# Attention, soft experts and a gated layer on one core: first loads in longer runs, two weights moved into attention

## The chip, the core and the metric

The kernel runs on one core of a Trainium2 chip. The core has TensorE (PE, matrix products, with its weight loads listed as PEld), VectorE (DVE), ScalarE (ACT), GpSimd (POOL) and SyncE (SP, which here only issues DMAs), an on-chip memory of 128 partitions (SBUF), and accumulators that only PE, DVE and ACT reach (PSUM). The metric is the time of one execution in device microseconds (us). Each engine takes its instructions strictly in the order in which the program lists them; a waiting instruction holds up everything behind it on its engine.

## The reference

Three layers follow each other; the output of one is the input of the next.

```
# attention: 4 batches, 12 heads, 448 tokens, 64 wide
scores = q @ k.T / 8;  masked above the diagonal
attn   = softmax(scores);  x = attn @ v            # -> x: 1792 x 768
# soft experts: 8 experts with 4 slots each, 1024 wide
logits = x @ phi                                   # 1792 x 32
d = softmax(logits over tokens);  slot_in = d.T @ x
slot_out[e] = relu(slot_in[e] @ w1[e]) @ w2[e]
x = softmax(logits over slots) @ slot_out
# gated layer: 1536 wide
out = (sigmoid(x @ w_gate) * (x @ w_val)) @ w_out
```

q, k, v, phi, w1 and w2 are 32-bit floats. The three gated weights come as 64-bit floats; the kernel reads them as 32-bit words and makes 32-bit floats of them on the chip.

## The kernel before

**Attention** works on 24 pairs of heads (six pairs per batch). q, k and v come in 12 groups of four heads, two pairs each. For a pair, PE turns q and k round (tile psT), ACT writes the scaled high half of them in 16 bits and DVE the low half (qT), PE makes the scores (psS), DVE masks them and finds row maxima (nm), ACT takes the exponentials (P), PE turns those round (psP), ACT or DVE copies them to PT, and PE multiplies with v (psV). The scale comes from sums of squares: `first_squares` for group 0, `squares_1` for group 1, both on DVE and ACT; from group 2 on POOL makes them (tiles sq and sqr), and a small product (psq) spreads the result. Group 0's q and k are fetched by `load_first`, one DMA per head, in runs of 256 bytes (a row of 64 floats).

**Experts.** Their weights are 32 tiles of 1.5 MB (two for w1, two for w2 of each expert), read by SP through `load_w` in the order of the list `worder` into a ring of buffers, `ring`: 3 of pool wpC and `NA` of pool wpA, 10 in all, filled during attention. When attention's own memory comes free, five more join the ring. The gated layer is cut into six units of 256 columns; a unit's three weights (o = w_out, v = w_val, g = w_gate) are 1.5 MB each too, and unit 0's three stand in `worder` ahead of expert 6. Right after expert 5, ACT (`a1`, `a2`) and DVE (`d1`, `d2`) make floats of these three tiles, in that order per tile, and the o tile is then split in two 16-bit halves: its largest value (`absw`) goes through a product of ones (`one`, tile amx on PE) and `pow2` (four short DVE instructions that make a power of two and its inverse) before `whi` and `wlo` write the halves.

**Gated layer.** For each unit, `psg` multiplies the experts' result with the g and v weights, `mv` finds the largest values, `one2` spreads them (amx), `pw2` makes powers of two, `gh` and `fld` fold the product, `sth` and `stl` store it in 16 bits (st). Then for each batch `gv` makes gate and value (psg, psv), ACT the sigmoid (sg), DVE the product (hs), ACT and POOL its halves (hhi, hlo), `outp` the products with w_out (pso), and ACT, DVE and POOL add them into oacc. The weights of the next unit are read and converted meanwhile.

**What sets the order.** Attention and the gated layer are each recorded as a list of operations with a cost, dependencies and a due time, and `Plan.play` puts them in order: of the operations that an engine could start within `WAIT` of the earliest, the one due first. The tables `SHIFT` (attention) and `GSHIFT` (gated layer) move due times by kind of operation; `SLACK`, `MARGIN`, `WAIT` and their `A` versions set the rest. The plan only sets an order: on the chip nothing is held until a planned time. The experts between them are ordered by the framework's scheduler. `keep_warm` puts products of ones (psf) that nobody reads where PE would be idle: around the end of attention and at the start of the gated layer.

Of the kernel before, what the change touches and what calls it, by code (L numbers as in the profile page):

```python
# [8 lines left out]
F32 = mybir.dt.float32  # L9
F16 = mybir.dt.float16  # L10
I32 = mybir.dt.int32
# [90 lines left out]
def kernel(  # L102
# [41 lines left out]
    for g, (b, h0, n) in enumerate(GRP):  # L144
        for o in range(0, n, 2):
# [17 lines left out]
    GSHIFT = {('a1', 1): 23.4, ('a1', 2): -6.21, ('a1', 3): 117.66, ('a1', 4): -5.02, ('a1', 5): 53.58, ('a2', 1):  # L163
              20.66, ('a2', 2): 118.34, ('a2', 3): 123.22, ('a2', 4): 79.78, ('a2', 5): 4.11, ('absw',): 36.12,
              ('addp', 1): 9.2, ('addp', 2): -5.3, ('addp', 3): -47.55, ('addp', 4): 58.74, ('am',): 1.36, ('am2',):
              -23.99, ('d1', 1): -180.16, ('d1', 2): 54.75, ('d1', 3): -2.65, ('d1', 4): -1.62, ('d1', 5): 30.01,
              ('d2', 1): 9.59, ('d2', 2): -33.11, ('d2', 3): -32.37, ('d2', 4): 8.67, ('d2', 5): 0.27, ('evict', 0):
              -148.33, ('evict', 1): -68.2, ('evict', 2): -111.03, ('evict', 3): -19.74, ('evict', 4): -31.48,
              ('evict', 5): 19.57, ('fl',): -9.57, ('fld',): 25.66, ('gh',): -29.78, ('gv', 0): -10.56, ('gv', 1):
              -235.77, ('gv', 2): -71.57, ('gv', 3): 21.32, ('gv', 4): 9.31, ('gv', 5): 8.04, ('hhi', 0): -461.87,  # L170
              ('hhi', 1): 83.0, ('hhi', 2): 5.44, ('hhi', 3): 25.33, ('hhi', 4): -7.65, ('hhi', 5): 9.17, ('hlo', 0):
              -0.95, ('hlo', 3): -9.74, ('hlo', 4): 42.9, ('hlo', 5): 20.64, ('hsv', 0): 17.3, ('hsv', 1): -5.98,
              ('hsv', 2): 0.18, ('hsv', 3): -20.78, ('hsv', 4): 18.54, ('hsv', 5): 4.2, ('ld', 1): -6.69, ('ld', 2):
              23.28, ('ld', 3): -32.29, ('ld', 4): -2.0, ('ld', 5): 39.32, ('mv',): -42.04, ('one',): -118.12,
              ('one2',): -17.53, ('outp', 0): 65.58, ('outp', 1): 1.02, ('outp', 10): 136.03, ('outp', 11): -0.62,
              ('outp', 12): -6.35, ('outp', 2): -3.63, ('outp', 3): 123.94, ('outp', 4): -8.45, ('outp', 5): -18.09,
              ('outp', 6): 218.04, ('outp', 7): -1.03, ('outp', 8): 231.97, ('outp', 9): 108.01, ('psg',): -384.17,
              ('pw',): -22.44, ('pw2',): -103.76, ('sig', 0): -240.48, ('sig', 1): -4.63, ('sig', 2): 27.87, ('sig',
              3): -144.49, ('sig', 4): -20.28, ('sig', 5): 17.06, ('sth', 0): -26.98, ('sth', 1): -11.12, ('sth', 2):
              -2.93, ('sth', 3): -40.58, ('sth', 4): -4.7, ('sth', 5): -0.58, ('stl', 0): 3.56, ('stl', 1): -0.2,  # L180
              ('stl', 2): 25.38, ('stl', 3): 8.1, ('stl', 4): -61.65, ('stl', 5): 13.43, ('store', 0): -10.25,
              ('store', 1): 15.69, ('store', 10): 2.55, ('store', 11): 55.39, ('store', 12): 11.05, ('store', 13):
              2.24, ('store', 2): 10.3, ('store', 3): 3.04, ('store', 4): -40.57, ('store', 5): 29.87, ('store', 6):
              7.57, ('store', 7): 43.43, ('store', 8): -4.75, ('store', 9): 49.48, ('whi',): -12.54, ('wlo',): 19.95}
    NFILL = 20
    AE = 9
    SQN = 32
    ASLACK, AMARGIN, AWAIT = 1.317, 1.41, 0.087
    PERIOD = 7.8
# [1114 lines left out]
```

## Time and profile before

| | us |
|---|---|
| three runs: median (lowest to highest) | 519.91 (519.75 to 521.16) |
| the profiled execution | 519.79 |
| its span in the profile | 518.0 |
| PE busy | 470.9 (91%) |
| DVE busy | 378.0 (73%) |
| ACT busy | 341.4 (66%) |
| POOL busy | 277.9 (54%) |

The span has four parts: the start until some 20 us, attention until 207, the experts until 300, the gated layer to the end. Shares of the whole span say little, since each part has another limit. An engine's idle time matters only if the part's limiting engine waits for it.

### The profile page before, as it was taken

What the parts mean: (1) busy time and instruction counts of PE and PEld (TensorE: products, weight loads), DVE (VectorE), ACT (ScalarE), POOL (GpSimd) and SP (SyncE); (2) the same over time, 40 slices, a digit from 0 to 9 for tenths busy, and PEclk for the clock granted to TensorE, in tenths of its full rate; (3) what the DMA queues carried; (4) which work ended last, traced back from release to release, by engine and by line L of the source; (5) the groups of instructions that cost most, each with busy time, mean ns of one, the idle gap of its engine ahead of it and who ended that gap; (6) DMA issues with size and microseconds to landing.
All of it is one profiled execution on the core that took longest, in us unless ns stands there. A gap on an engine that the chain in (4) does not pass through costs nothing.

```text
span 518.0 us, 12116 instructions
## 1 busy us (share of the span) xinstructions
PE 470.9 (91%) x4516; PEld 293.0 (57%) x4516; DVE 378.0 (73%) x920; ACT 341.4 (66%) x759; POOL 277.9 (54%) x371
## 2 busy tenths in 40 slices
PE   3899999999999999999837578999999998999997
PEld 2667767767667776655412234555455554555554
DVE  3889888989988987621055049899798998978564
ACT  3788887989887886111081059999897897686330
POOL 3088777787768812000000007249699997997530
PEclk9999999999999999999985999999999999999999
DMA  6866776762767357899999993360553320300145
GB/s 149 200 167 190 202 218 156 176 186 62 220 154 191 123 154 279 331 416 424 410 409 424 412 395 139 114 253 0 163 204 121 139 106 1 124 0 1 53 178 196
DMA packets 87531, 101.55 MB, mean 196 GB/s; under 512 B 68656, under 2 KB 68912, under 8 KB 85424
## 3 DMA queue, kind: packets, MB, share of 16 engines
q1 hardware_dynamic: 86544, 100.55, 57.4%
q8 instruction: 35, 0.57, 0.5%
q10 hardware_dynamic: 928, 0.23, 0.2%
q14 instruction: 24, 0.20, 0.1%
HBM read 95.26 MB, written 5.51 MB: 195 GB/s over the span
## 4 chain that ended last, share of the span: by engine, by line
PE 54%; POOL 15%; DMA 12%; DVE 6%; ACT 6%; issue 6%; SPq 1%; POOLq 0%; ACTq 0%; DVEq 0%
PE pso L244 11%; PE psP L244 8%; PE psS L244 8%; PE psV L244 7%; DMA w<-in_moe_w_gate_dram 5%; POOL hlo L244 5%; POOL oacc L244 5%; DMA w<-in_moe_w_dram 5%; POOL sq L244 4%; PE so L1069 3%; PE psT L244 3%; PE psh L1056 3%; PE psY L244 2%; PE psX L244 2%; ACT w L244 2%
## 5 line engine op out<-in xcount | busy, mean ns | idle before, releaser
L244 POOL TENSOR_TENSOR hlo<-hs,hhi 128x448 f16<-128x448 f32 x47 | 69.8, 1494 | 124.7 <-ACT hhi L244 124.6
L244 PEld LDWEIGHTS <-hhi 128*128 128x128 f16 x672 | 65.2, 98 | 51.1 <-issue 7.9
L244 ACT ACTIVATE P<-psS,nm 128x384 f32<-128x384 f32 (+3 forms) x168 | 82.1, 505 | 11.4 <-DVE nm L244 8.7
L244 PE MATMUL pso<-wh,hhi 128*128 128x384 f16 x336 | 82.7, 326 | 1.0 <-ACT oacc L244 0.5
L244 POOL TENSOR_TENSOR oacc<-oacc,ev 128x384 f32<-128x384 f32 x56 | 76.4, 1381 | 11.7 <-ACT ev L244 10.3
L244 PE MATMUL pso<-wh,hlo 128*128 128x384 f16 x336 | 81.6, 326 | 0.9 <-POOL hlo L244 0.9
L244 PE MATMUL pso<-wl,hhi 128*128 128x384 f16 x336 | 82.4, 326 | 0.0
L244 DVE CUSTOM_DVE_ANT_0 psS<-psS,cmaskq,sc 128x128 f32<-128x128 f32 (+2 forms) x144 | 62.8, 487 | 3.1 <-PE psS L244 2.4
L244 DVE SCALAR_TENSOR_TENSOR oacc<-pso,osc,oacc 128x384 f32<-128x384 f32 x84 | 50.1, 611 | 18.5 <-PE pso L244 18.2
L244 DVE SCALAR_TENSOR_TENSOR w<-w 128x1536 int32<-128x1536 int32 x30 | 62.0, 2067 | 0.7 <-ACT w L244 0.7
L244 PE MATMUL psP<-ident,P 128*128 128x128 f32 x384 | 59.4, 282 | 1.3 <-ACT P L244 1.3
L244 POOL TENSOR_TENSOR sq<-sq 112x512 bf16<-112x512 bf16 (+1 forms) x80 | 51.1, 639 | 6.0
L244 PEld LDWEIGHTS psP<-ident,P 128*128 128x128 f32 x384 | 42.9, 142 | 15.2 <-issue 8.8
L244 ACT COPY PT<-psP 128x512 f32<-128x512 f32 x83 | 46.7, 587 | 6.3 <-PE psV L244 5.2
L244 PE MATMUL psS<-qT,qT 64*64 64x256 f16 (+3 forms) x1008 | 48.9, 294 | 1.5 <-ACT qT L244 0.7
L244 ACT ACTIVATE w<-w 128x1536 int32<-128x1536 uint16 (+1 forms) x30 | 49.3, 1647 | 1.3 <-DMA w<-in_moe_w_gate_dram 1.3
L244 PE MATMUL psV<-PT,v 128*64 128x448 f32 (+3 forms) x384 | 46.8, 386 | 0.0
L244 ACT ACTIVATE ev<-pso,osc 128x384 f32<-128x384 f32 x56 | 32.7, 584 | 21.1 <-PE pso L244 11.1
L244 PEld LDWEIGHTS <-hlo 128*128 128x128 f16 x336 | 32.7, 98 | 23.2 <-POOL hlo L244 1.3
L327 DVE TENSOR_SCALAR hm<-psh,emask 128x256 f32<-128x256 f32 x8 | 5.3, 662 | 46.7 <-PE psh L1056 44.2
L244 PEld LDWEIGHTS <-qT 64*64 64x64 f16 x1008 | 28.2, 108 | 19.5 <-issue 7.0
L1064 ACT COPY hT<-psht 128x256 f32<-128x256 f32 x8 | 3.0, 372 | 53.6 <-PE psht L1062 46.8
(252 smaller groups left out, 847.7 us busy)
## 6 DMA issues: line engine op xcount, KB each, us to landing
w<-in_moe_w_dram SPq DMA_DIRECT2D x32, 1536.0 KB, 9.5
w<-in_moe_w_out_dram SPq DMA_DIRECT2D x6, 1536.0 KB, 11.8
w<-in_moe_w_val_dram SPq DMA_DIRECT2D x6, 1536.0 KB, 13.6
w<-in_moe_w_gate_dram SPq DMA_DIRECT2D x6, 1536.0 KB, 6.6
q<-in_q_dram SPq DMA_DIRECT2D x48, 112.0 KB, 3.3
k<-in_k_dram SPq DMA_DIRECT2D x46, 112.0 KB, 3.4
out_dram<-oacc SPq DMA_DIRECT2D x13, 384.0 KB, 2.3
v<-in_v_dram SPq DMA_DIRECT2D x36, 128.0 KB, 3.2
```

The source lines that it names most:

```text
L244: x = f(*a, **kw)
L327: nc.vector.tensor_scalar(to.rearrange("s (i q) -> s q i", i=2), ps.rearrange("s (q i) -> s q i", i=2), 0.0, emask[:, e:e + 1], ALU.max, A ...
L1056: nc.tensor.matmul(ps[32 * g:32 * g + 32, :], lhsT=slotT[:, kc, :], rhs=w[:, kc % 3, 256 * g:256 * g + 256], start=kc == 0, stop=kc == KC - 1)
L1064: nc.scalar.copy(hT, pt)
L1069: nc.tensor.matmul(so[32 * c:32 * c + 32, :], lhsT=hT[:, i, 32 * g:32 * g + 32], rhs=w[:, f % 4, 256 * c:256 * c + 256], start=e == 0 and ...
```

## The change

- `load_first` fetches group 0's q and k with one DMA for two heads, in runs of 1 KB: a partition's four rows of one head lie behind each other, so the tile is ordered by head and then by row (`by_head`). Both k DMAs are issued on ACT's queue. `st_T` for group 0 then takes eight products with the unit matrix, each 64 wide, where it took four transposes.
- 25 times two products of ones (operations `fs`) stand between the first instructions of PE.
- `worder` starts with unit 0's v and g, ahead of all experts; only o stays ahead of expert 6. Pool wpA has 6 buffers (was 7), and the 12 KB per partition go to a tile `first`, which holds the converted v and g. `convert` does what `a1`, `a2`, `d1`, `d2` do, in thirds of a tile, as operations of attention's plan (`cv`). The plan now has 11 loads: v, g and 9 expert tiles.
- The last expert tile is loaded by two DMAs of half a tile.
- `pow2` computes in place in PSUM and copies the power out at the end (`pw3` for a unit's g and v). `mv` writes 16 bits itself, so `am2` is gone; `am` moves from DVE to ACT; `fld` is recorded behind `one2`.
- All numbers of both tables, the six slack figures and some costs differ.

```diff
-    NA, NB, NC, ND = 7, 4, 3, 2
+    NA, NB, NC, ND = 6, 4, 3, 2
+    NV = 2
+    NFIRST = 25
-    SLACK, MARGIN, WAIT = 1.252, 0.894, 0.49
+    SLACK, MARGIN, WAIT = 0.213, 0.838, 0.347
-    ASLACK, AMARGIN, AWAIT = 1.317, 1.41, 0.087
+    ASLACK, AMARGIN, AWAIT = 0.573, 1.325, 0.083
...
+    first = bctx.enter_context(tc.tile_pool(name="first", side="right", bufs=1)).tile([128, 2, KC, UC], F32, name="first")
...
+        m, r = mx[:, :n], mx[:, n:]
-        on.ve.tensor_scalar(p, mx, 2.0 ** -20, None, ALU.max)
-        on.ve.tensor_scalar(p.bitcast(I32), p.bitcast(I32), 0x7F800000, None, ALU.bitwise_and)
-        on.ve.reciprocal(s, p)
-        on.ve.tensor_scalar(s, s, P14, None, ALU.mult)
-        return p, s
+        on.ve.tensor_scalar(m, m, 2.0 ** -20, None, ALU.max)
+        on.ve.tensor_scalar(m.bitcast(I32), m.bitcast(I32), 0x7F800000, None, ALU.bitwise_and)
+        on.ve.reciprocal(r, m)
+        on.ve.tensor_scalar(s, r, P14, None, ALU.mult)
+        return p, s, lambda: on.ve.tensor_copy(p, m)
...
-    worder = []
+    worder = w_unit(0)[1:]
-            worder += w_unit(0)
+            worder += w_unit(0)[:1]
...
+            last = key == ("2", E - 1, 1)
+            for x, y in [(to[:, z], src[:, z]) for z in range(2)] if last else [(to, src)]:
+                Pinned(nc.sync).dma_start(out=x, in_=y)
...
-                rows_in(ac if w and not o else sp, qkbuf[0][w][:, :, o * D:(o + 2) * D], src[0, o:o + 2])
+                to = by_head(w)[:, o:o + 2]
+                (ac if w else sp).dma_start(out=to.rearrange("p h j d -> p h (j d)"), in_=src[0, o:o + 2].rearrange("h (p j) d -> p h (j d)", j=RJ))
...
+            if g == 0:
+                for j in range(RJ):
+                    for h in range(2):
+                        te.matmul(ps[64 * h:64 * h + 64, RP * j:RP * j + RP], lhsT=by_head(w)[:, o + h, j], rhs=ident[:RP, :RP], start=True, stop=True)
+                return
...
+        def convert(nm, z, m):
+            t, x = wt[nm, 0], slice(2 * z, 2 * z + 2)
+            lo, hi = (t.bitcast(I32).rearrange("p a (b w) -> p a b w", w=2)[:, x, :, y] for y in range(2))
+            top = t.bitcast(U16).rearrange("p a (b w) -> p a b w", w=4)[:, x, :, 1]
+            if m == 0:
+                ac.activation(out=lo, in_=top, func=AF.Copy, scale=2.0 ** -13, bias=2.0 ** -15 - 0.5)
+            elif m == 1:
+                ac.activation(out=hi.bitcast(F32), in_=hi.bitcast(F32), func=AF.Copy, scale=2.0 ** -112)
+            elif m == 2:
+                ve.scalar_tensor_tensor(lo, hi, -2 ** 31, lo, ALU.bitwise_and, ALU.bitwise_or)
+            else:
+                ve.scalar_tensor_tensor(w32[nm, 0][:, x].bitcast(I32), hi, 3, lo, ALU.logical_shift_left, ALU.bitwise_or)
...
+        for n in range(NFIRST):
+            op(("fs", n), plain(keep_warm, n, 2), {"P": 0.21}, [], first=3.0 + 0.28 * n if n < 5 else 6.6 + 0.33 * (n - 5), new=[] if n else [("p", ("fs",))], use=[("fs",)] if n else [],
+               behind=[("fs", n - 1)] if n else [])
+        for n in range(NC + NA + NV):
+            op(("w", n), lambda e: load_w(), {"D": 1.3}, [("cv", n - NC - NA, z, 3) for z in range(3)] if n >= NC + NA else [], lag=6.5,
+               first=19.0 + 15.3 * n)
+            if n < NV:
+                for z in range(3):
+                    for m in range(4):
+                        op(("cv", n, z, m), plain(convert, "vg"[n], z, m), {"A": 0.69} if m < 2 else {"V": 0.62}, [("cv", n, z, m - 1) if m else ("w", n)])
...
-        on.ve.tensor_copy(x, unit[u]["m", nm])
+        on.ac.copy(x, unit[u]["m", nm])
...
-        d["mgv"] = sm2.tile([128, 2], F32, tag="mgv", name="mgv")
+        d["mgv"] = sm2.tile([128, 2], BF16, tag="mgv", name="mgv")
...
-            for nm in "ovg":
-                for f in (a1, a2, d1, d2):
-                    f((nm, 0))
+            for f in (a1, a2, d1, d2):
+                f(("o", 0))
...
-        op((fld, u), call(fld), {"P": 0.9}, [(gh, u)], new=[("a", p2)], use=[h])
-        op((am2, u), call(am2), {"V": 0.15}, [(mv, u)])
-        op((one2, u), call(one2), {"P": 0.04}, [(am2, u)], new=[("b", x)])
+        op((one2, u), call(one2), {"P": 0.04}, [(mv, u)], new=[("b", x)])
+        op((fld, u), call(fld), {"P": 0.9}, [(gh, u)], new=[("a", p2)], use=[h], behind=[(one2, u)])
         op((pw2, u), call(pw2), {"V": 0.8}, [(one2, u)], use=[x])
+        op((pw3, u), call(pw3), {"V": 0.42}, [(pw2, u)], use=[x])
```

PE's first instructions before the change (psT is q or k turned round, am the squares' sums, qT the 16-bit halves):

```order
L244 MATMUL psT<-ident,q_91 128x112 x4
L244 MATMUL psT<-ident,k_95 128x112 x4
L244 LDWEIGHTS avgb
L244 MATMUL psq<-am_241,avgb 128x2
L244 LDWEIGHTS avgb
L244 MATMUL psq<-am_260,avgb 128x2
L244 LDWEIGHTS qT_103
L244 MATMUL psS<-qT_119,qT_103 64x256
```

The same place after it, from the last of ten products of ones that now stand first:

```order
L248 MATMUL psf<-ones 128x256
L248 MATMUL psT<-ident,q_95 64x112 x8
L248 LDWEIGHTS avgb
L248 MATMUL psq<-am_253,avgb 128x2
L248 MATMUL psT<-ident,k_99 64x112 x8
L248 LDWEIGHTS ones
L248 MATMUL psf<-ones 128x256
L248 LDWEIGHTS ones
L248 MATMUL psf<-ones 128x256
```

Ten products of ones stand ahead of the first psT, six behind the second, eight between the second psq and the scores, and 26 more up to the second part of pair 0's scores.

ACT in the fourth pair of attention, after the change (w is the v weight's tile, P the exponentials, yt a copy for the logits); before, the rows of w are not there:

```order
L248 ACTIVATE P_139,sum<-psS,nm 128x128
L248 ACTIVATE P_141,sum<-psS,nm 128x256
L248 ACTIVATE w<-w 128x512
L248 ACTIVATE P_140,sum<-psS,nm 128x128
L248 ACTIVATE P_142,sum<-psS,nm 128x256
L248 COPY PT<-psP 128x2x2x128
L248 ACTIVATE w<-w 128x512 x2
L248 COPY yt<-psY 128x448
L248 ACTIVATE P_145,sum<-psS,nm 128x448
```

The twelve instructions of `convert` on ACT stand from the fourth to the ninth pair, DVE's twelve from the fifth to about the eleventh.

PE at the start of the gated layer before the change (psg is first the product, then its fold by `fld`; amx is `one2`):

```order
L995 MATMUL psg<-w,soT 32x256 x12
L244 LDWEIGHTS ones
L244 MATMUL psf<-ones 128x256
L244 MATMUL psg_4744<-gh,fold_66 128x512
L244 LDWEIGHTS ones
L244 MATMUL amx_4751<-am_4749,ones 128x2
```

And after it, with the last of seven products of ones:

```order
L1036 MATMUL psg<-first,soT 32x256 x12
L248 LDWEIGHTS ones
L248 MATMUL psf<-ones 128x256
L248 LDWEIGHTS ones
L248 MATMUL amx_4836<-mgv,ones 128x2
L248 MATMUL psg_4838<-gh,fold_70 128x512
```

`one2` has moved ahead of `fld`.

## Rows read from the trace of the kernel before

**Rows 1.** Busy time of each engine by stretch (start:end, length, then us).

```profile
core 0: us, PE busy (x) PEld busy (x) DVE busy (x) ACT busy (x) POOL busy (x), PEclk, DMA share, GB/s
10.80:20.50 9.70, 7.87 (x65) 5.40 (x64) 7.01 (x24) 5.59 (x18) 0.00 (x0) 1.00 0.79 170
20.50:36.00 15.50, 15.50 (x188) 10.65 (x188) 14.00 (x50) 13.42 (x43) 9.74 (x16) 1.00 0.66 184
36.00:82.00 46.00, 44.84 (x562) 32.56 (x562) 40.34 (x141) 39.10 (x120) 36.26 (x68) 1.00 0.69 188
82.00:207.00 125.00, 124.06 (x1499) 87.49 (x1495) 106.73 (x365) 104.44 (x315) 81.79 (x159) 1.00 0.62 174
...
217.80:297.60 79.80, 59.88 (x759) 31.20 (x751) 22.28 (x36) 17.51 (x22) 0.55 (x1) 0.89 1.00 407
...
307.40:345.00 37.60, 35.30 (x216) 19.04 (x217) 33.59 (x50) 35.21 (x50) 16.24 (x9) 1.00 0.49 177
345.00:470.00 125.00, 119.33 (x761) 67.30 (x760) 110.77 (x162) 102.04 (x149) 110.21 (x77) 1.00 0.28 99
```

**Rows 2.** SP's issues at the start, in order of time (start, us).

```profile
0.73 2.95 SPq L244 DMA_DIRECT2D q<-in_q_dram  x4
3.73 1.29 SPq L244 DMA_DIRECT2D k<-in_k_dram  x2
...
19.43 2.57 SPq L244 DMA_DIRECT2D q<-in_q_dram  x4
```

**Rows 3.** The chain that ended last, from 20 to 40 us (start, us).

```profile
21.39 4.12 DMA q<-in_q_dram
...
36.99 0.19 PE psq L244
```

**Rows 4.** PE from 10 to 24 us in order of time.

```profile
10.83 2.08 PE L244 MATMUL psS<-qT,qT 64*64 64x256 f16 x26 [0.35 <-DVE qT L244]
12.84 1.01 PE L244 MATMUL psT<-ident,k 112*128 112x112 f32 x4
...
22.14 0.69 PE L244 MATMUL psS<-qT,qT 64*64 64x256 f16 x24
...
23.25 0.55 PE L244 MATMUL psT<-ident,k 112*128 112x112 f32 x4
```

**Rows 5.** Groups of instructions from 260 to 280 us (count, busy us, mean ns).

```profile
L316 DVE SCALAR_TENSOR_TENSOR w<-w 128x1536 int32<-128x1536 int32 x3 | 5.3, 1757 | 6.1 <-ACT w L263 6.1
...
L308 ACT ACTIVATE w<-w 128x1536 int32<-128x1536 uint16 x3 | 5.0, 1671 | 0.0
L263 ACT ACTIVATE w<-w 128x1536 f32<-128x1536 f32 x3 | 4.9, 1640 | 0.0
```

**Rows 6.** PE from 260 to 300 us in order of time.

```profile
270.47 0.19 PE L977 MATMUL amx<-am,ones 128*128 128x1 bf16 x1 [6.52 <-DVE am L973]
271.40 2.79 PE L1056 MATMUL psh<-w,slotT 128*32 128x256 f32 x24 [0.74 <-DMA w<-in_moe_w_dram]
...
290.06 1.50 PE L1056 MATMUL psh<-w,slotT 128*32 128x256 f32 x24 [1.75 <-DMA w<-in_moe_w_dram]
...
293.93 1.93 PE L1069 MATMUL so<-w,hT 128*32 128x256 f32 x24 [1.15 <-DMA w<-in_moe_w_dram]
297.62 1.93 PE L1069 MATMUL so<-w,hT 128*32 128x256 f32 x24 [1.77 <-DMA w<-in_moe_w_dram]
```

**Rows 7.** All engines at the start of the gated layer, in order of time.

```profile
303.32 0.58 ACT L244 COPY gh<-psg 128x512 f32<-128x512 f32 x1 [10.08 <-DVE mgv L244]
303.80 1.59 ACT L244 ACTIVATE w<-w 128x1536 int32<-128x1536 uint16 x1
303.96 1.13 PE L244 MATMUL psg<-gh,fold 128*128 128x512 f32 x2 [0.93 <-ACT gh L244]
304.92 0.17 PE L244 MATMUL amx<-am,ones 128*128 128x2 bf16 x1
...
306.02 0.84 ACT L244 ACTIVATE st<-psg,gv0s 128x256 f16<-128x256 f32 x2 [0.62 <-DVE ag L244]
```

More of the change, by code (lines that the diff above doesn't have):

```diff
@@ L286 @@
     wt = {}
-    w32 = {}
+    w32 = {("g", 0): first[:, 0], ("v", 0): first[:, 1]}
     ring = [wpC] * NC + [wpA] * NA
@@ L788, in group @@
                         op(("am", o, w), plain(first_squares, o, w), {"VA"[w]: 0.65}, [("ld", 0, o)], new=[("sq", ("sq", 0))] if first else [],
-                           use=[] if first else [("sq", 0)], behind=[] if first else [("am", 0, 0)])
+                           use=[] if first else [("sq", 0)], behind=[] if first else [("am", 0, 0)] if w or not o else [("sc", 0, 0)])
                     op(("am16", o), plain(first_cast, 0, o), {"V": 0.17}, [("am", o, 0), ("am", o, 1)])
@@ L825, in pair @@
                 x, y, z = ("T", i, w), ("hi", i, w), ("lo", i, w)
-                op(x, plain(st_T, i, w), {"P": 0.4}, [("ld", 0, o) if g == 0 else ("ld", g, w)], new=[("s", x)], use=[(n, g)],
-                   behind=[("S", i - 1, 0)] if i else [])
+                op(x, plain(st_T, i, w), {"P": 0.4 if g else 0.78}, [("ld", 0, o) if g == 0 else ("ld", g, w)], new=[("s", x)], use=[(n, g)],
+                   behind=[("S", i - 1, 0)] if i else [("psq", 0, 0)] if w else [])
                 op(y, plain(st_hi, i, w), {"A": 0.52}, [x, got], new=[(f"hi{w}", y)], use=[x, sg])
@@ L972, in am @@
         x = unit[u]["am", nm] = sm2.tile([128, 1], BF16, tag="am" + nm, name="am")
-        on.ve.tensor_copy(x, unit[u]["m", nm])
+        on.ac.copy(x, unit[u]["m", nm])
     def one(nm, u):
-        x = unit[u]["x", nm] = ps1.tile([128, 1], F32, tag="b" if nm == "v" else "a", name="amx")
-        on.te.matmul(x, lhsT=ones, rhs=unit[u]["am", nm], start=True, stop=True)
+        x = unit[u]["x", nm] = ps1.tile([128, 2], F32, tag="b" if nm == "v" else "a", name="amx")
+        on.te.matmul(x[:, :1], lhsT=ones, rhs=unit[u]["am", nm], start=True, stop=True)
     def pw(nm, u):
         d = unit[u]
-        d["p", nm], d["s", nm] = pow2(sm2, d.pop(("x", nm)), 1, f"{nm}{u}")
+        d["p", nm], d["s", nm], f = pow2(sm2, d.pop(("x", nm)), 1, f"{nm}{u}")
+        f()
     def whi(u, e):
@@ L999, in mv, with pw3 @@
         d = unit[u]
-        d["mgv"] = sm2.tile([128, 2], F32, tag="mgv", name="mgv")
+        d["mgv"] = sm2.tile([128, 2], BF16, tag="mgv", name="mgv")
         on.ve.tensor_reduce(d["mgv"], d["ps"], axis=AX.X, op=ALU.max, apply_absolute_value=True)
-    def am2(u):
-        x = unit[u]["am2"] = sm2.tile([128, 2], BF16, tag="am2", name="am2")
-        on.ve.tensor_copy(x, unit[u]["mgv"])
     def one2(u):
-        x = unit[u]["x2"] = ps1.tile([128, 2], F32, tag="b", name="amx2")
-        on.te.matmul(x, lhsT=ones, rhs=unit[u]["am2"], start=True, stop=True)
+        x = unit[u]["x2"] = ps1.tile([128, 4], F32, tag="b", name="amx2")
+        on.te.matmul(x[:, :2], lhsT=ones, rhs=unit[u]["mgv"], start=True, stop=True)
     def pw2(u):
         d = unit[u]
-        p, r = pow2(sm2, d.pop("x2"), 2, f"gv{u}")
+        d["pgv"], r, d["f"] = pow2(sm2, d.pop("x2"), 2, f"gv{u}")
         for c, nm in enumerate("gv"):
-            d["p", nm], d["s", nm] = p[:, c:c + 1], r[:, c:c + 1]
+            d["s", nm] = r[:, c:c + 1]
+    def pw3(u):
+        d = unit[u]
+        d.pop("f")()
+        p = d["pgv"]
+        for c, nm in enumerate("gv"):
+            d["p", nm] = p[:, c:c + 1]
         d["ag"] = sm1(f"ag{u}")
@@ L1265 @@
                 if a:
[L1266 removed]
+                    op((addp, n) + k, call(addp), {"G": 1.36}, [(evict, n) + k], use=[("ev", n) + k], due=now + 2.5)
             if u == NU - 1:
```

88 lines of the change are left out of this document (43 added, 45 removed), and 29 rows, old and new, of tables (GSHIFT, SHIFT).

## The prediction

> **What bounds the kernel now.** I read the table of stretches first, then the order of time at the three seams (start, end of the experts, start of the gated layer), and last the chain for what leads into attention.
>
> In attention PE is the bound. From 20.5 to 82 us it is idle for 1.2 of 61.5 us and from 82 to 207 for 0.9 of 125, while DVE and ACT are idle for 10 to 15% [rows 1]. So what delays the first pairs delays everything, and what is added on DVE and ACT is free only as long as it fits into their idle time.
>
> Before that, the start has two limits. SP issues without a pause: the DMAs of group 0 take it until 5.0 us, and the q load of group 2 goes out from 19.43 to 22.0 [rows 2], lands at 25.5, and POOL's squares of that group end in PE's psq at 36.99 [rows 3]. And PE is slow: the column of the granted clock reads 1.00 there [rows 1], but 26 score products take 2.08 us at 10.83 and 24 of them 0.69 at 22.14, and the same four transposes 1.01 at 12.84 and 0.55 at 23.25 [rows 4]. By its durations PE runs on its lower level (1.2 GHz) until about 20 us; it had been busy only in pieces before.
>
> In the experts DMA is the bound: from 217.8 to 297.6 its share is 1.00 at 407 GB/s [rows 1], and at the end PE waits for each tile: its work starts at 290.06, 293.93 and 297.62, each time released by a weight's DMA [rows 6]. That is 3.78 us for a tile of 1.57 MB.
>
> In the gated layer PE is nearly the bound: it is idle for 2.3 us from 307.4 to 345 and for 5.7 of 125 from 345 to 470 [rows 1]. From 307.4 to 345 ACT (35.2 of 37.6) and DVE (33.6) are as full.
>
> **The change part by part.**
>
> *The start.* SP issued six DMAs for group 0, 2.95 + 1.29 = 4.24 us [rows 2]. Now it issues two, and ACT's queue the other two. At 0.65 to 0.74 each that is 1.4 us, so all later issues up to group 2's q move ahead by 2.8 us, and with it POOL's squares and the psq at 37. PE must gain as much, or that is hidden. Its work between 10.8 and 20.5 was 7.87 us [rows 1] on the lower level; on the upper one it is about half, 3.9 less. Against this, the four transposes of a tile become eight products with the unit matrix, which no row shows. By bounds: 0.55 (as the transposes) to 1.1 (double); I take 0.8, being nearer to a full product, so that the second pair's two tiles cost 0.5 more on PE. The 50 products of ones stand in PE's queue ahead of real work: 26 of them between the first pair's scores and the next ones, some 3 us even on the upper level, in a stretch in which PE waited 1.8 of 9.7 us before. So PE's gain is 3.9 - 0.5 - 1 = 2.4 plus what the earlier landing gives. I take SP's 2.8. If the products hold up real work, 0.5 is left; if both limits fall together, 4.5 is gained.
>
> *Conversions in attention.* Unit 0's v and g are converted in thirds: 6 instructions of each of four kinds. A third of 1.671 and 1.640 is 0.56 and 0.55, of DVE's 1.757 it is 0.59 [rows 5]: 6.6 us on ACT and 7.0 on DVE (d2 as d1), and with what a short instruction costs by itself up to 8 each. They stand in the fourth to about the eleventh pair. From 36 to 82 us ACT is idle for 6.9 us and DVE for 5.7 [rows 1]; from 82 to 207 in all for 20.6 and 18.3. So they use up the idle time of the stretch in which they stand and a little more, on the two engines that feed PE. That cover is incomplete: I take 2.0 us lost on PE. If all of it fits, nothing; if one engine's addition is fully exposed, 7. The first conversion also waits for the landing of the v weight with pair 3's exponentials behind it on ACT; the first weight's load went out right after group 2's q, at 22.0, and the conversion stands behind all of pair 2's work, so I expect no wait.
>
> *One tile less at the end of the experts.* Before, 10 tiles were loaded within attention and 25 of 35 were left: 22 of experts and three of unit 0. Now 11 are loaded and 24 are left. The buffers that the rest goes into are as many at each moment, counted from the end: 15 before less the extra load, 14 now. DMA being full [rows 1], one tile less is 3.75 us, if PE keeps up. It does, as far as the rows go. Expert 6 stands behind amx, where the conversion of o ends; PE waited 6.5 us for it [rows 6]. Counted back from 271.40 by 3.78 a tile (expert 6's first, g, v, o), o landed at about 260.1 and amx came 10.4 later; now o lands at 263.8, and expert 6 starts at about 274 at the latest. The last tile lands at 293.9 (on the old scale). That leaves 20 us for two experts, which on the upper level need under 9 each (four times 1.5 to 1.93 and some 2 for the turn between them).
>
> *The last tile in halves.* PE started its 24 products (1.93 us) when the whole tile had landed [rows 6]. Half of them can now go before: 0.96 gained.
>
> The Trainium skill speaks against this edit: "DMA: Bandwidth & Descriptors", section "Anatomy of one DMA", gives each DMA a fixed cost of about 2 us beside its bytes. By that rule, if the two halves ran one after the other, this term would be a loss of about 1 us. The rows show nothing of it between queued loads: a tile every 3.78 us is 415 GB/s, all of it bytes [rows 6].
>
> *Start of the gated layer.* amx went over PE behind the fold, at 304.92, and only then the four short DVE steps began; st followed at 306.02 [rows 7]. Now amx can go right behind mv (gh was released by mgv at 303.32), so the fold is what is late: it ends at 305.05. But on ACT the conversion of unit 1's first tile stands between gh and st in both orders, until 305.39 [rows 7]. So st moves from 306.02 to about 305.45: 0.6 gained. The short steps now work in PSUM; what that costs no row shows, but the fold covers it up to 0.8 us.
>
> *The rest of the gated layer.* The same instructions, except that five 16-bit copies are gone from DVE, five move to ACT, and one short copy per scale comes; the new tables put everything in another order. PE's 8.0 idle us are all there is to gain. Which order is better is not to be seen in the trace, so both signs are open: from 4 us gained (half of the idle time) to 2 lost. I take 1.0 gained, since PE's waits for amx, the one wait that the change shortens by structure, are a small part of it.
>
> **Sum**, against the profiled execution (519.79 us: 518.0 of span and 1.79 around it; the median of the runs is 519.91, so the two are the same): 519.79 - 2.8 + 2.0 - 3.75 - 0.96 - 0.6 - 1.0 = 512.7 us.
>
> **Rivals.**
>
> *The seams and the orders give more.* Both limits of the start fall together (4.5), the conversions fit (0), and the gated layer regains half its idle time (4.0): 519.79 - 4.5 - 3.75 - 0.96 - 0.6 - 4.0 = 506.0. For it: the idle time of ACT and DVE in all of attention is twice what is added. Against: it asks for every free term at its good end.
>
> *Attention takes back most of it.* The start gains 1.0 and the conversions cost 5: 519.79 - 1.0 + 5 - 3.75 - 0.96 - 0.6 - 1.0 = 517.5. For it: in the stretch where they stand, ACT and DVE together have 12.6 us idle for 13.6 to 16 [rows 1, 5], and PE has four score buffers to live on.
>
> *PE becomes the bound of the last experts.* PE idles from 264 until amx, now some 10 us, and before, 24 products of psh took 2.79 us at 271.40 where they take 1.50 at 290.06 [rows 6]: the lower level. If PE stays there through experts 6 and 7, each takes about 13.8 us (four times 2.8 to 3.0, and 2.2 for the turn), and from 273.5 they end at 301.1, where they ended at 299.6. The tile and the half tile are lost and 1.5 more: 512.7 + 4.7 + 1.5 = 518.9. Against: before, PE was back on the upper level in time for expert 7.
>
> *Slower.* The conversions make ACT and DVE the bound of attention: each piece stands in order ahead of exponentials or masks that PE needs, and the two engines take turns in delaying it. All 13.6 us are then on the path: 519.79 + 13.6 - 2.8 - 3.75 - 0.96 - 0.6 - 1.0 = 524.3. It decides from the point at which PE loses more than 9.1 us in pairs 4 to 11. Against: PE has other pairs' work to do meanwhile, and both engines do have idle time.
>
> **How the numbers follow.** Chances: forecast 0.52 (its own range 509 to 516, from the bounds of start, conversions and orders, taken half way), more 0.20, attention takes back 0.17, PE bound in the last experts 0.05, slower 0.06. The range goes from the second case, a little below, to the third, a little above: 505.5 to 518. A measurement of this kernel tells 0.3% (1.6 us) from no change. Below 518.35 lie the first two cases and most of the third (0.14), 0.86; within 0.3% the rest of the third, the fourth and 0.01 of the last, 0.09; above, the last, 0.05.
>
> **What the profile after would show.** Start: group 0's DMAs issued by 2.2 us, first scores before 10.3, 24 score products in 0.7 us rather than 1.9, group 2's psq at 34 rather than 37. Conversions: some 2 us more PE idle from 36 to 98. Experts: the DMA share still 1.00, the last psh and so starts 3.7 us apart and the last run of so 12 products long. Gated layer: amx ahead of the fold. It would be wrong if attention ended later than 208 us, if PE did not wait for the last tiles, or if PE's idle time in the gated layer were far from 7 us.

## The result, and the profile after

The changed kernel takes 511.0 us (median of four runs, 510.1 to 511.9); the kernel before takes 520.4 beside it (four runs, 519.8 to 521.2). The ratio is 0.9826, with a 95% interval of 0.980 to 0.985. The prediction was 512.7 with a range of 505.5 to 518: direction and size were right. Three of its terms were not, and their errors nearly cancelled.

The span fell from 518.0 to 508.7 us. I cut it at five instructions that both kernels have: psl, with which the logits of the last batch are turned round at the end of attention; PE's start on the last expert tile (in the changed kernel on its second half); psst, which turns the experts' result; the first psg of the gated layer; and the end.

| stretch | before, us | after, us | difference |
|---|---|---|---|
| start to psl | 210.64 | 212.02 | +1.38 |
| psl to the work on the last expert tile | 86.98 | 82.36 | -4.62 |
| from there to psst | 2.46 | 1.60 | -0.86 |
| psst to the first psg of the gated layer | 7.35 | 6.54 | -0.81 |
| from there to the end | 210.57 | 206.18 | -4.39 |

In these two traces attention, then, ends later than before, and more is gained behind it than I had forecast. The two upper rows are the less certain ones: over the traces below of kernels with the same attention, psl moves by 3.1 us and the stretch behind it by 2.5. The same stretches as in [rows 1], of the changed kernel (columns as there; the last two start where its gated layer starts):

```profile
36.00:82.00 46.00, 44.26 (x521) 30.90 (x521) 44.67 (x142) 43.45 (x130) 37.69 (x62) 1.00 0.66 181
82.00:207.00 125.00, 124.06 (x1518) 87.61 (x1514) 114.43 (x375) 100.95 (x310) 83.51 (x160) 1.00 0.63 182
...
302.50:340.00 37.50, 34.47 (x209) 18.73 (x210) 33.06 (x47) 34.92 (x51) 17.54 (x10) 1.00 0.60 223
340.00:465.00 125.00, 123.88 (x796) 70.71 (x794) 109.50 (x167) 106.06 (x160) 113.24 (x80) 1.00 0.26 92
```

From 36 to 82 us DVE (44.67 of 46) and ACT (43.45) are nearly full, and PE's idle time rises only from 1.16 to 1.74 us. In the gated layer PE's idle time goes from 5.67 to 1.12 us in 125.

SP's issues at the start (start, us), which answer to [rows 2], and what SP waited for in the first 20 us:

```profile
8.76 2.39 SPq L248 DMA_DIRECT2D v<-in_v_dram  x4
12.09 3.03 SPq L248 DMA_DIRECT2D k<-in_k_dram  x4
15.17 2.38 SPq L248 DMA_DIRECT2D v<-in_v_dram  x4
17.66 2.58 SPq L248 DMA_DIRECT2D q<-in_q_dram  x4
```

```profile
SPq L248 <- PE psS L248: 1.1, 2, 0.6
SPq L248 <- PE psT L248: 0.9, 1, 0.9
```

SP is free at 11.15 and stands still until PE reads group 0's k for pair 1 (psT), because group 2's k goes into the same buffer; another 0.4 us is lost while the four DMAs of that k go out (3.03 us, 2.60 before). Group 2's q is issued at 17.66, 1.77 us earlier than in [rows 2], where I had counted on 2.8; its psq comes at 35.03 (36.99 in [rows 3]).

PE's products that spread the scales, psq, for groups 3 to 5 (order of time; in brackets how long PE had waited, and for what):

```profile
51.11 0.19 PE L248 MATMUL psq<-sqr,avgb 112*128 112x64 bf16 x1 [0.53 <-POOL sqr L248]
...
68.09 0.19 PE L248 MATMUL psq<-sqr,avgb 112*128 112x64 bf16 x1 [0.56 <-POOL sqr L248]
...
85.12 0.19 PE L248 MATMUL psq<-sqr,avgb 112*128 112x64 bf16 x1 [0.53 <-POOL sqr L248]
```

PE waits for POOL three times in a row, 17.0 us apart, where the conversions stand. The waits are short, but the chain that ended last agrees: from 36 to 90 us POOL's squares and sums (sq) are 27.9% of it. Group 3's part of that chain (start, us):

```profile
44.82 2.05 POOL sq L248 x2
...
49.25 0.78 POOL sq L248
50.10 0.64 POOL sq L248
50.81 0.25 POOL sqr L248
51.11 0.19 PE psq L248
```

Experts and prologue, on PE:

```profile
290.68 2.86 PE L1113 MATMUL so<-w,hT 128*32 128x256 f32 x36 [1.13 <-DMA w<-in_moe_w_dram]
294.38 1.06 PE L1113 MATMUL so<-w,hT 128*32 128x256 f32 x12 [0.83 <-DMA w<-in_moe_w_dram]
...
299.13 0.16 PE L248 MATMUL amx<-mgv,ones 128*128 128x2 bf16 x1
299.79 1.12 PE L248 MATMUL psg<-gh,fold 128*128 128x512 f32 x2 [0.50 <-ACT gh L248]
...
302.52 0.36 PE L248 MATMUL psg<-cT,st 128*128 128x448 f16 x1 [0.18 <-DVE st L248]
```

Against [rows 6, 7]: PE still waits for the last tiles, the last run of so is 12 products long, and amx stands ahead of the fold.

### The profile page after: what moved, and what is told of

It is laid out like the page before. It is cut to its first block, busy times and chain, and to the rows that moved or that the text cites. A ratio compares the mean times of both kernels' runs of the same rounds, so it can differ in the third digit from the quotient of the medians.

```text
span 508.7 us, 12285 instructions
## 1 busy us (share of the span) xinstructions
PE 475.8 (94%) x4614; PEld 297.9 (59%) x4614; DVE 379.8 (75%) x928; ACT 340.3 (67%) x772; POOL 283.7 (56%) x372
## 4 chain that ended last, share of the span: by engine, by line
PE 56%; POOL 15%; DVE 9%; DMA 7%; ACT 6%; issue 5%; SPq 1%; POOLq 0%; ACTq 0%; DVEq 0%
PE pso L248 16%; PE psP L248 6%; PE psS L248 6%; PE psV L248 6%; POOL hlo L248 5%; DMA w<-in_moe_w_dram 5%; POOL sq L248 5%; POOL oacc L248 5%; PE so L1113 4%; PE psT L248 4%; PE psh L1100 3%; PE psY L248 2%; DVE psS L248 2%; PE psX L248 2%; PE psg L248 2%
## 5 line engine op out<-in xcount | busy, mean ns | idle before, releaser
L248 POOL TENSOR_TENSOR hlo<-hs,hhi 128x448 f16<-128x448 f32 x48 | 71.7, 1504 | 111.6 <-ACT hhi L248 111.2
L248 DVE SCALAR_TENSOR_TENSOR w<-w 128x1536 int32<-128x1536 int32 (+1 forms) x36 | 69.3, 1926 | 0.4 <-ACT w L248 0.3
L248 DVE CUSTOM_DVE_ANT_0 psS<-psS,cmaskq,sc 128x128 f32<-128x128 f32 (+2 forms) x144 | 62.9, 488 | 1.9 <-PE psS L248 1.2
L248 POOL TENSOR_TENSOR sq<-sq 112x512 bf16<-112x512 bf16 (+1 forms) x80 | 55.3, 691 | 6.3
L248 ACT ACTIVATE w<-w 128x1536 int32<-128x1536 uint16 (+3 forms) x42 | 57.3, 1382 | 1.3 <-DMA w<-in_moe_w_gate_dram 1.3
L248 PE MATMUL psP<-ident,P 128*128 128x128 f32 x384 | 54.6, 278 | 0.3 <-ACT PT L248 0.3
L248 ACT COPY PT<-psP 128x512 f32<-128x512 f32 x67 | 38.8, 600 | 3.7 <-PE psP L248 2.6
L248 PEld LDWEIGHTS psV<-PT,v 128*64 128x64 f32 x384 | 25.4, 136 | 22.5 <-issue 14.0
```

The lines of the kernel that those rows point to most:

```text
L248: x = f(*a, **kw)
```

## The experiments

Each starts from the changed kernel unless said otherwise. Ratios are to the kernel before, run on the same chip. Places such as psl are read from one profiled execution of each kernel, times are medians. Six kernels with the same attention as the changed one (itself and the collision kernel below among them) had psl at 210.7 to 213.8 us, 211.9 on average, and POOL's sq at 11.0 to 27.9% of the chain from 36 to 90 us: a microsecond at psl says nothing, and three say something only together with the times.

**The conversions left out.**

```diff
         def convert(nm, z, m):
+            return
...
         pa.play()
+        nc.gpsimd.memset(first, 0.0)
```

> The 24 pieces of the conversion in attention are left out (unit 0's gate and value weights are zero, so the gated layer of unit 0 computes with zeros); every other instruction of attention stands in its place. Theory A (the 2.4 us that attention lost from pair 1's scores to psl are the conversions'): psl at 209.6 us instead of 212.0 and the time 508.6 (ratio 0.978). Theory B (the other order of attention costs it, not the pieces): psl stays at 211.5 to 212 and the time at 510.5 to 511. Theory C (the pieces cost more than shown, and the new order alone would have gained): psl at 207 to 208.5, the time 506 to 507.5.

Measured: 506.9 us, ratio 0.977 (0.974 to 0.979); psl at 208.8. The time is theory C's, psl lies between A and C: the pieces cost 3.2 us at psl (against 212.0) and 4.1 in the median. POOL's row on the sums of group 3's k, in the changed kernel and then here:

```profile
46.94 3.80 POOL L248 TENSOR_TENSOR sq<-sq 112x512 bf16<-112x512 bf16 x4
```

```profile
48.32 2.79 POOL L248 TENSOR_TENSOR sq<-sq 112x512 bf16<-112x512 bf16 x4
```

The pieces are on ACT and DVE, and POOL's own instructions become 1.0 us shorter when they go. PE no longer waits for POOL, nothing of POOL is left in the chain from 36 to 90 us, and psq of groups 2 to 5 is 15.3 to 15.8 us apart (16.1 to 17.0 with the pieces).

**VectorE's pieces with one operand instead of two.**

```diff
-                ve.scalar_tensor_tensor(lo, hi, -2 ** 31, lo, ALU.bitwise_and, ALU.bitwise_or)
+                ve.tensor_scalar(lo, hi, 3, None, ALU.logical_shift_left)
...
-                ve.scalar_tensor_tensor(w32[nm, 0][:, x].bitcast(I32), hi, 3, lo, ALU.logical_shift_left, ALU.bitwise_or)
+                ve.tensor_scalar(w32[nm, 0][:, x].bitcast(I32), hi, 3, None, ALU.logical_shift_left)
```

> The changed kernel with VectorE's twelve pieces of the conversion replaced, each in its place, by an instruction of the same 128 x 512 words with one operand in SBUF instead of two (a shift alone; unit 0's gate and value weights are then not the reference's). All other instructions and their order are the same. In the changed kernel four of POOL's sums take 3.80 us instead of 2.79 beside the pieces. Theory A (the second SBUF operand holds POOL up, and POOL is late for psq): the sums take 2.8 to 2.9, psq of groups 2 to 5 are 15.3 to 15.8 us apart instead of 16.1 to 17.0, PE's waits for POOL are gone, psl comes at 209 to 209.8 instead of 211.6, and the time is 507.5 to 509. Theory B (VectorE's own time is what costs): the pieces take 0.6 to 0.7 us each, and psl stays within 0.6 of 211.6, the time 510 to 511.5. Theory C (ACT's twelve pieces are the cost, beside VectorE's): as B, with POOL's sums at 2.8 and no waits for POOL.

Measured: 507.7 us, ratio 0.978 (0.976 to 0.980); psl at 208.0. Its stretch from 36 to 82 us, and the same sums on POOL:

```profile
36.00:82.00 46.00, 45.75 (x528) 31.94 (x521) 44.44 (x147) 45.01 (x134) 37.90 (x66) 1.00 0.68 187
```

```profile
46.18 2.99 POOL L248 TENSOR_TENSOR sq<-sq 112x512 bf16<-112x512 bf16 x4
```

This decides for theory A, though psl came earlier than it said and the last of the three gaps of psq is 16.6 us. DVE (44.44 us, third figure) and ACT (45.01) are as full as in the changed kernel, and yet PE is idle for 0.25 us instead of 1.74, does not wait for POOL, and the whole loss is gone; the chain from 36 to 90 us holds nothing of POOL here either. So it is the second operand that costs. The new instructions are also shorter (0.66 and 0.75 us instead of 0.92 and 1.02); the next run shows that the old ones, too, take only 0.69 where POOL is idle. How much of the loss comes over POOL's late psq and how much over DVE's longer pieces is not measured apart; the chain speaks for POOL.

**The collision by itself.** In the experts, where both engines have little to do:

```diff
+        if 3 <= e <= 5:
...
+            if e != 3:
+                Pinned(nc.gpsimd).tensor_tensor(scr[:, :256], hm, hm, ALU.mult)
+            for n in range(6):
+                if e != 4:
...
+                    Pinned(nc.vector).scalar_tensor_tensor(lo, hi, 0, lo, ALU.bitwise_and, ALU.bitwise_or)
+                if e != 3:
+                    Pinned(nc.gpsimd).tensor_tensor(scr, po_x, po_x, ALU.mult)
```

> The disputed cost by itself: in the changed kernel, in the experts, where POOL and VectorE have little to do and DMA sets the pace, VectorE does six pieces of the size of the conversion's (two operands in SBUF, 128 x 512 words, the result equal to the input) behind expert 3 with POOL idle; POOL does six squares of 128 x 512 behind expert 4 with VectorE nearly idle; both at once behind expert 5. Theory A (they hold each other up): the piece takes 0.6 us alone and 0.9 to 1.1 beside POOL, a square 1.0 alone and 1.5 to 1.7 beside VectorE, together as long as one after the other. Theory B (the piece is just dear at this size, with its strided words): 0.9 to 1.0 us in both places, and a square 1.0 in both. The time is to stay within 1 us of the changed kernel's.

DVE's pieces behind expert 3 (alone) and expert 5 (beside POOL), then POOL's squares behind expert 4 (alone) and expert 5:

```profile
245.86 4.33 DVE L248 SCALAR_TENSOR_TENSOR first<-first 128x512 int32<-128x512 int32 x6
...
266.55 7.48 DVE L248 SCALAR_TENSOR_TENSOR first<-first 128x512 int32<-128x512 int32 x6
```

```profile
259.49 6.63 POOL L248 TENSOR_TENSOR scr<-first 128x512 bf16<-128x512 f32 x6
...
267.77 9.66 POOL L248 TENSOR_TENSOR scr<-first 128x512 bf16<-128x512 f32 x6
```

Of those behind expert 5 the last four pieces and the first four squares stood fully side by side (count, busy us, mean ns):

```profile
L248 DVE SCALAR_TENSOR_TENSOR first<-first 128x512 int32<-128x512 int32 x4 | 5.6, 1411 | 0.1
L248 POOL TENSOR_TENSOR scr<-first 128x512 bf16<-128x512 f32 x4 | 5.5, 1368 | 0.3
```

Alone, a piece takes 0.69 us and a square 1.04; side by side 1.41 and 1.37. Theory A holds in kind. The time was 515.4 us (one run), not within 1 us: the pieces behind expert 5 also held up o's conversion, amx came at 281.0 instead of 273.0, and psl was already 1.8 us later in this execution, at 213.8 with the same attention.

**The conversions moved to later pairs.** The pieces are hung behind exponentials and masks of pairs 11 to 17, all else in its place.

```diff
-                        op(("cv", n, z, m), plain(convert, "vg"[n], z, m), ...
+                        op(("cv", n, z, m), lambda e: None, ...
...
+        for s in range(6):
+            todo = [plain(convert, "vg"[s // 3], s % 3, m) for m in range(4)]
+            for at in (("e", 11 + s, 1, 0), ("e", 11 + s, NQ, 0), ("m", 12 + s, 1, 0), ("m", 12 + s, NQ, 0)):
+                x = pa.ops[pa.at[at]]
+                x.f = lambda e, f=x.f, todo=todo, at=at: (f(e), todo.pop(0)(e))
```

> The changed kernel with all 24 pieces of the conversion moved: ACT's from the fourth to ninth pair to pairs 11 to 16, VectorE's to pairs 12 to 17; every other instruction of attention stays in its place. In the changed kernel POOL's squares and sums of a group take longer while the pieces stand on VectorE (four sums 3.80 us instead of 2.79), groups follow each other every 17.0 us instead of 15.3, and PE waits 0.5 us for POOL in three of them. Theory A (POOL is what the conversions cost: it has no slack in the first groups and 1.0 to 2.2 us a group in the later ones): psq of groups 2 to 5 is 15.3 to 16 us apart, PE does not wait for POOL there, psl comes at 209 to 210.3 instead of 211.6 (mean of five runs with the same attention), the time is 508.5 to 509.8 us (ratio 0.979 to 0.982 of what runs beside it). Theory B (the idle time of ACT and VectorE is used up, wherever the pieces stand, my theory in the prediction): psl at 211 to 212.5, 510.5 to 512. Theory C (the later pairs have less room, and the moved pieces wait there): above 512.

Measured: 514.4 us, ratio 0.991 (0.989 to 0.993); psl at 215.2. Groups 2 to 6 recover as theory A says (psq 15.3 to 16.2 us apart), but the next three gaps are 18.0, 17.7 and 19.6. PE's waits from 98 to 153.5 us (total, times, longest):

```profile
PE psV L248 <- issue: 1.4, 1, 1.4
PE psT L248 <- ACT P L248: 1.2, 3, 0.5
PE psV L248 <- DVE xn L248: 0.6, 1, 0.6
PE psq L248 <- POOL sqr L248: 0.5, 1, 0.5
```

The first of them, at psV, shows no releaser. So the time is theory C's: hung on by hand, among exponentials that PE needs, the pieces cost more than at the plan's places. But from 98 to 156 us POOL's sq is 16.3% of the chain again, so the collision went along, and the two are not told apart. Whether a plan that knows of the collision would find room there is open.

**The first loads.** Undone in the changed kernel (runs of 256 bytes, four transposes):

```diff
-                (ac if w else sp).dma_start(out=to.rearrange("p h j d -> p h (j d)"), in_=src[0, o:o + 2].rearrange("h (p j) d -> p h (j d)", j=RJ))
+                rows_in(ac if w and not o else sp, qkbuf[0][w][:, :, o * D:(o + 2) * D], src[0, o:o + 2])
```

> The first loads go back to runs of 256 bytes, one DMA per head, five of them... on the queue of SP as before the change, and the four transposes instead of eight products; everything else as changed. Theory A (my term for the start: SP's issues set the time of group 2's psq, 2.8 us later without the change): psq at 37 to 37.8 instead of 35.0, psV of pair 2 again at 40 to 41, the time 512.5 to 514 us (ratio 0.985 to 0.989). Theory B (the start is set by PE from 4.6 us on, and the later landing falls into its slack): psq moves, but the middle of attention does not, and the time is 511 to 511.5.

Six DMAs, not five, are on SP's queue. Measured: 514.5 us, ratio 0.991 (0.988 to 0.994); group 2's q is issued at 20.44, its psq comes at 37.28, after a wait of PE of 2.32 us, and psl at 215.0. Theory A, with a time a little above its range: 2.78 us on SP's queue become 3.0 at psl and 3.4 in the median. The other side, these loads alone in the kernel before (the same edit the other way round):

> The kernel before, with nothing of the change but the first loads: two DMAs of 1 KB runs on each of two queues, the tile ordered by head, and the eight products instead of four transposes. No products of ones, the old tables. Theory A (SP's issues are the limit of the start, as my first term had it): group 2's psq at 34 to 34.5 instead of 36.99 and psl at 207.8 to 208.8 instead of 210.6, the time 517 to 518 (ratio 0.994 to 0.996). Theory B (the load alone is worth less, because PE stays on the lower level until 20 us without the products of ones): psq at 34 to 35, psl at 209.8 to 210.6, 519 to 520.

Measured: 519.8 us, ratio 1.001 (0.999 to 1.003); psl at 210.4: theory B, though for another reason than the level. SP there:

```profile
8.93 2.36 SPq L244 DMA_DIRECT2D v<-in_v_dram  x4
13.31 2.63 SPq L244 DMA_DIRECT2D k<-in_k_dram  x4
...
19.38 1.91 SPq L244 DMA_DIRECT2D q<-in_q_dram  x3
```

SP waits 2.0 us for PE's psT of pair 1's k and another 0.6 for its psP, and group 2's q goes out at 19.38, 0.05 us before [rows 2]. Its psq comes at 36.08, not at 34 to 35 as both theories had it. In the old order the loads alone gain nothing that the time shows.

**The products of ones.** Left out altogether, and cut to the first 24:

```diff
-            op(("fs", n), plain(keep_warm, n, 2), {"P": 0.21}, ...
+            op(("fs", n), lambda e: None, {"P": 0.21}, ...
```

```diff
+            op(("fs", n), plain(keep_warm, n, 2) if n < 12 else (lambda e: None), {"P": 0.21}, ...
```

> The 50 products of ones at the start are left out; nothing else changes on PE, and nothing else is left out. Theory A (the products are there for TensorE's level and pay for themselves): the first pairs run on the lower level again, 24 scores of pair 0 take about 2 us instead of 1.26 for 30, the eleven scores of pair 1 that stood at 19.44 us come at 20.5 or later, the time is 512 to 513 us (ratio 0.984 to 0.987). Theory B (they stand in the way of real work, as the chain of the changed kernel suggests, where PE is never idle from 4.6 us on): those scores come at 18.5 and the time is 510 us (ratio 0.980). In both, group 2's psq stays at 35.0, since POOL and the queues do not change.

> Only the first 24 of the 50 products of ones are kept: those ahead of pair 0's scores. Theory A (the later 26 keep the level up while PE waits for ACT and DVE): without them PE falls back between 11 and 20 us, four turns of a k tile take over 1 us again where they took 0.5 to 1.0, and the time is 511.5 to 512.5. Theory B (the later ones only hold up real work): pair 1's scores come 0.5 to 1.0 us earlier than 19.44 and the time is 510 to 510.5. Group 2's psq stays at 35.0 in both.

Measured: 511.0 and 511.5 us, both 0.984 (0.982 to 0.987 and 0.981 to 0.988); psl at 212.0 and 211.9. Without them pair 0's 26 scores take 2.08 us (30 took 1.26 with them), by that duration the lower level, and pair 1's eleven scores still come earlier than with them:

```profile
9.50 2.08 PE L248 MATMUL psS<-qT,qT 64*64 64x256 f16 x26 [0.29 <-DVE qT L248]
...
18.65 0.68 PE L248 MATMUL psS<-qT,qT 64*64 64x384 f16 x11 [0.76 <-ACT P L248]
...
35.88 0.19 PE L248 MATMUL psq<-sqr,avgb 112*128 112x64 bf16 x1 [1.47 <-POOL sqr L248]
```

They were 19.44 with all 50. But PE then waits 1.47 us for group 2's psq, which comes 0.85 later, though both theories had it unmoved, because SP gets group 2's k later. With the first 24 kept, pair 1's scores come at 18.86, and its k and q take 0.99 us to turn as with all 50: PE does not fall back without the other 26. At psl nothing is left of any of this, and the products are worth nothing that these runs can tell.

**The last tile in one DMA.**

```diff
-            last = key == ("2", E - 1, 1)
+            last = False
```

> The last expert tile in one DMA again; nothing else. Theory A (the halves gain what 12 products take): the last run of so is 24 products long, it begins with the tile's landing, and everything behind it comes 0.9 to 1.0 us later; the time is 512. Theory B (each DMA has a fixed cost that runs after the one before it): the one DMA lands earlier than the second half did, by some 2 us, and the time is 510.

Measured: 511.7 us, ratio 0.987 (0.985 to 0.989).

```profile
290.50 1.93 PE L1113 MATMUL so<-w,hT 128*32 128x256 f32 x24 [1.15 <-DMA w<-in_moe_w_dram]
294.19 1.93 PE L1113 MATMUL so<-w,hT 128*32 128x256 f32 x24 [1.76 <-DMA w<-in_moe_w_dram]
```

From there to psst it is 2.46 us, in halves 1.60 from the second half's landing. Counted from PE's start on the tile before, which a landing releases too, PE starts on the whole tile 3.69 us later and on the second half 3.70. Theory A.

**The gated layer's steps and tables, apart.** The steps are those of the diff (powers in PSUM, `mv` in 16 bits, `am` on ACT, `one2` ahead of `fld`); the tables are `GSHIFT`, the three figures beside it and five costs. Three kernels, each with one of the two or both put back:

```diff
-    SLACK, MARGIN, WAIT = 0.213, 0.838, 0.347
+    SLACK, MARGIN, WAIT = 1.252, 0.894, 0.49
...
-        op((fld, u), call(fld), {"P": 0.9}, [(gh, u)], new=[("a", p2)], use=[h], behind=[(one2, u)])
+        op((fld, u), call(fld), {"P": 0.9}, [(gh, u)], new=[("a", p2)], use=[h])
+        op((am2, u), call(am2), {"V": 0.15}, [(mv, u)])
```

> The changed kernel with the gated layer of before: its short scale steps in SBUF, the 16-bit copies on VectorE, the fold recorded ahead of the spreading product, and the table, the slack figures and the costs of before. Attention, its conversions, the loads and the last tile in halves stay changed. Theory A (the 4.4 us between the first gv and the end of the span are the gated layer's own): 210 to 211 us from the first gv to the end instead of 206.2, and the prologue 0.6 to 0.9 longer: 515 to 516.5 us (ratio 0.990 to 0.993). Theory B (something ahead of it gives the gain, unit 0's weights being ready sooner): still 206 to 207.5, the time 511 to 512.5.

> The steps of the gated layer as changed (PSUM, amx ahead of the fold), but with the table, slack figures and costs of before. Theory A (the steps give the gain: fewer instructions on VectorE, the shorter way to the scales): 206 to 207.5 us from the first gv to the end, the time 511 to 512.5. Theory B (the order that the tables set gives it): 209 to 210.5, the time 514 to 515.5. My prediction had 1.0 us for both together and held the waits for amx, the part that the steps shorten, for a small one.

> The steps of the gated layer of before (SBUF, the 16-bit copies on VectorE, the fold ahead of the spreading product), with the table, slack figures and costs as changed. Theory A (steps): 209 to 210.5 us from the first gv to the end, the time 514 to 515.5. Theory B (order): 206 to 207.5 and 511.5 to 513, the prologue alone being 0.6 to 0.9 longer.

| us (ratio with interval); first psg to the end | old tables | new tables |
|---|---|---|
| old steps | 516.2 (0.992 to 0.996); 210.9 | 524.9 (1.008 to 1.014); 219.4 |
| new steps | 514.7 (0.990 to 0.995); 210.8 | 511.0 (0.980 to 0.985); 206.2 |

psst to the first psg takes 7.29 us with the old steps in either table, 6.54 to 6.56 with the new ones. PE's longest waits in the gated layer, with old steps and new tables:

```profile
PE psv L248 <- DVE hs L248: 4.4, 5, 1.5
PE pso L248 <- DVE oacc L248: 1.7, 3, 0.8
PE pso L248 <- DVE wl L248: 1.4, 1, 1.4
```

with new steps and old tables, and with both new:

```profile
PE psv L248 <- DVE hs L248: 3.3, 4, 1.5
PE pso L248 <- POOL hlo L248: 2.0, 2, 1.1
PE pso L248 <- ACT ev L248: 1.6, 2, 1.3
```

```profile
PE psv L248 <- DVE hs L248: 1.7, 2, 1.4
PE pso L248 <- DVE oacc L248: 0.4, 2, 0.2
```

Neither theory alone: the steps gain 0.7 in the prologue and nothing behind it, the tables without their steps lose 8.5, and only together do they gain the 4.4. A table of due times fits one list of instructions. With old steps and new tables one stall is dear: PE is idle for 3.5 us from 480 to 490, and its granted clock (seventh figure) falls behind it (stretches as above):

```profile
480.00:490.00 10.00, 6.47 (x34) 3.20 (x33) 6.05 (x13) 7.47 (x13) 8.14 (x7) 0.90 0.00 0
490.00:500.00 10.00, 10.00 (x49) 5.34 (x48) 4.59 (x9) 0.80 (x2) 2.02 (x2) 0.76 0.26 103
500.00:510.00 10.00, 10.00 (x63) 6.04 (x62) 5.96 (x11) 0.00 (x0) 0.00 (x0) 1.00 0.54 208
```

PE is full from 490 to 500 and does 49 products there instead of 63; 14 products are 2.2 us at the later pace.

## Why the prediction was right, and where not

**The start (forecast -2.8).** The issues fell as computed, but "all later issues up to group 2's q move ahead by 2.8 us" failed: SP now waits 0.9 us for PE's psT of pair 1's k, which in the kernel before was done while SP was still busy, and loses another 0.4 in the issues behind it. I checked what lies behind the removed issues and not what the first of them overwrites. Left: 1.77 at the issue of q, 1.96 at psq. With the conversions' effect away, psl comes 1.8 to 2.6 us earlier than before; the new order of attention is part of that, and no run has the old table of attention with the rest of the change. The price of the 256-byte runs in the changed order, 3.0, does bear out the size. What I had counted for PE, 3.9 gained by the upper level and 1 lost to the products of ones, decided nothing: without those products the time is the same.

**Conversions (forecast +2.0).** The amount was too low and the mechanism wrong: "they use up the idle time of the stretch in which they stand". They cost 3 to 4 us, and what costs is not the idle time that they fill but the collision of their second operand with POOL. POOL makes the squares of the next group with no slack in the first groups; two-operand pieces on DVE lengthen its sums, psq comes late, and PE with it. The trace of before held a sign of it: POOL's sums are 10.5% of the chain from 36 to 90 us, but I had followed the chain only to 40. The durations were too low as well, 0.92 and 1.02 us instead of 0.59: [rows 5] was taken where POOL does nothing (a piece of this size takes 0.69 there). The slower rival rested on the same wrong account.

The Trainium skill has this, in "SBUF — State Buffer", section "Who interferes with whom": a VectorE instruction with two SBUF inputs contends with a GpSimd instruction that reads SBUF, since its second input comes through the read interface that both use. The runs agree (one input: sums of 2.8 to 3.3 us, two: 2.8 to 3.8, none: 2.8). They differ on the same page's rule in "Summary: rules for kernel authors", that the second of the two to issue blocks fully: from 266.6 to 274.0 us six pieces and somewhat over four squares were done in 7.5 us that take 8.8 one after the other.

**One tile less (forecast -3.75).** PE waited for the last tiles, as the forecast needs, and the rival in which PE sets the end did not come about. Measured from psl it is 4.6 us in the two traces of the table. The 0.9 more than a tile are no finding: in the traces with the changed order of weights the stretch from psl to the last tile takes 82.0 to 84.9 us, in the two with the old order 86.6 and 87.0, so the gain is 1.7 to 4.9 us, with 3.75 inside, and no run has this edit alone.

**The halves (forecast -0.96)** gained 0.86, and no loss of a DMA's fixed cost shows: the second half lands when the whole tile does (3.70 and 3.69 us behind the tile before). I had stretched the Trainium skill there: "DMA: Bandwidth & Descriptors", section "Anatomy of one DMA", fits its 2 us to DMAs issued by GpSimd and puts them down mostly to the report of the last byte. Here SP issued, and the queued halves did not pay it one after the other. **The prologue (forecast -0.6)** gained 0.81, of which 0.7 are the steps' by the 2x2; amx went ahead of the fold as read.

**The rest of the gated layer (forecast -1.0)** gained 4.4. The failed step is "both signs are open ... I take 1.0": 4 us, half of PE's idle time, was my best case. That the waits for amx are few was no argument, because the gain needs both changes: neither the steps nor the tables bring any of it behind the prologue without the other. Which operations the tables moved to that effect is not shown.

So the total is off by 2.2 us of 9.3 while single terms are off by 0.8, 1.6 and 3.4 (and one by the 0.9 that is no finding). Two of my three signs of a wrong forecast did appear: attention ended later than 208, and PE's idle time in the gated layer was far from 7. That the number survived is luck: attention and the gated layer pulled in opposite ways.

## What to carry to other kernels

Before instructions go into the idle time of an engine, look at every engine that shares something with it: here DVE and ACT had most of the time, and POOL, on neither's list, paid. When issues are taken out of a queue, ask what the next transfer overwrites and when that was last read; the freed time ends there. And a hand-tuned table of an order belongs to its list of instructions: judged alone, or kept when the list changes, it can lose more than the edit gains.

## What the hardware showed beside this

In four of the traces PE's last 48 products of the experts (so) were slow without any change there. They take 3.65 us at 261.7 in the changed kernel, at a granted clock of 1.00. At the end of the experts they took 5.34 us at a granted clock of 0.68 with the old gated layer, 5.58 at 0.65 with the old first loads, 5.21 at 0.69 without the products of ones and 5.16 at 0.71 with the loads alone in the kernel before: part of each ran on the lower of PE's two levels (1.2 and 2.4 GHz). PE had waited 1.9 to 2.2 us for a tile shortly before in all four; but so it had with the last tile in one DMA (2.2 us), where the clock stayed at 1.00. So the rival in which PE sets the end is near.

How much of the 514.5 and 516.2 us of two of these kernels this is can't be said: those are medians, and the traces are of executions of 516.8 and 517.9 us, the longest of each. In both, amx comes 62.9 and 63.1 us behind psl instead of 61.0, which is before the slow products; with the conversions moved it is 63.5, and there the last products run at a granted clock of 1.00. What delays amx is open. The stages of these kernels were therefore compared at psl and behind psst.
